# Longer rows and fewer transfers under way in a scan with a mixture of adapters

## The chip, the core and the metric

The kernel runs on one core of a Trainium2 chip. Its engines are TensorE (PE, matmuls, and PEld, the loads of their stationary operand), VectorE (DVE), ScalarE (ACT), GpSimd (POOL) and SyncE (SP), which here only issues transfers. Sixteen DMA engines move data between the chip's main memory (HBM) and the on-chip memory SBUF; matmuls write to PSUM, which has eight banks. The metric is the device time of one execution in microseconds.

## What is computed

Two stages over 8 sequences of 6400 positions with 128 features. The first is a linear recurrence along each sequence:

```python
for t in range(S):
    h = a[:, t] * h + b[:, t]
    out[:, t] = h
```

The second treats all 51,200 positions as rows `x` of 128 features. Each row picks two of 8 adapters by its logits, and adds their weighted outputs:

```python
logits = x @ w_gate                       # (N, 8)
topk = the two largest of each row; w = softmax over those two
delta[row] += w[row, k] * ((x[row] @ A[e]) @ B[e])     # A[e]: 128 x 16, B[e]: 16 x 128
return x + delta
```

Inputs a and b and the output are float32, 26.2 MB each. Every position of a and b is read once and every position of the output is written once.

## The kernel before

The rows are cut into 100 chunks of 512 positions (C), and each chunk into 4 blocks of 128 (J). A chunk goes through these steps; the short names are those of the operations in the order lists:

- `la`, `lb` (line 396): transfers of a and b from HBM into `a_tm` and `b_tm`. From chunk 4 on (HEAD) two chunks come in one transfer, laid out as `(p j) d -> p j d`: each of the 128 partitions gets 8 consecutive positions, a row of 4 KB. The first four chunks come singly, in rows of 2 KB. There are six buffers of two chunks for each input (NL).
- `P` (line 417): PE turns positions into columns, because the scan runs along the free dimension. In a pair, chunk h lies in partitions 64h to 64h+63, so its transposes use half of the array's rows. A `P` weaves the 8 half transposes of b of chunk c with the 8 of a of chunk c+1, which use the other half. They go into PSUM banks `pB` and `pA`, two of each.
- `ae` (line 435): ACT copies a from `pA` into one of three tiles `a_st` of one chunk.
- `sc` (line 482): DVE scans the chunk, from `a_st` and `pB`, into `xT` (float16, features in partitions, positions in columns; NX chunks of room).
- `Z`, `ze` (lines 500, 506): for a unit of 4 or 6 blocks, PE multiplies x by the 8 adapters' A and by the gate in one matmul of 136 columns; ACT copies the result to `zl` (room for NZ blocks).
- `g1` to `g8`, `gx`, `w1` (lines 534 to 554): DVE, POOL and ACT find the two largest logits and the weights, for a group of up to 4 units.
- `mu` (line 569): POOL, sometimes DVE, multiplies z by the weights.
- `T`, `te` (lines 578, 300): PE transposes the weighted z, and ACT or DVE copies it to `zwT`.
- `D`, `oe` (lines 588, 589, 300): PE adds x, transposed back, and the adapters' outputs in a bank of `pO`; ACT, sometimes DVE, copies it to `outt` (room for NO blocks).
- `st` (line 631): a transfer of two chunks (the last four singly) from `outt` to HBM. Which blocks an output row takes follows from the layout of the store: `xT` is read in steps so that block b holds every eighth position of a pair.

The order of the work on each engine is written out by hand-given lists, `ORDER`, one for each engine (SyncE's list holds nearly all transfers). `Program.waits` derives from them and from each operation's dependencies which semaphores it waits for. An engine does its list in order: a transfer that waits on SyncE holds up all behind it. A load waits until the transposes of the former content of its buffer are done, a store until its `oe` copies are done, and an `oe` until the former store of its place has landed. `fi` are filler transposes that only keep PE at work between chunks 7 and 14.

`SPLIT` cuts the store of chunks 68 and 69 into two transfers of 124 and 4 partitions.

Of the kernel before, what the change touches and what calls it, by code (L numbers as in the profile page):

```python
# [7 lines left out]
F32 = mybir.dt.float32  # L8
# [18 lines left out]
TAIL_CHUNKS = 12  # L27
ORDER = {
# [16 lines left out]
    ),  # L45
    "act": (
# [16 lines left out]
    ),  # L63
    "dve": (
# [14 lines left out]
    ),  # L79
    "pool": (  # L80
# [100 lines left out]
def bass_associative_scan_2x2__then__mixture_of_adapters_kernel(  # L181
# [56 lines left out]
    with ExitStack() as stack:  # L238
# [140 lines left out]
        def woven(c):  # L379
            return c >= HEAD  # L380

        def load(c, n):
            p, h = c // HC, c % HC
            sl = p % NL
            for o_l, o_t, key, tile, src in ((o_la, o_A, "la", a_tm, af), (o_lb, o_B, "lb", b_tm, bf)):
# [13 lines left out]
                for k in range(n):  # L399
                    o_l[c + k] = op  # L400
# [330 lines left out]
```

## Time and profile before

| what | value |
|---|---|
| median of 3 runs | 201.11 us (200.93 to 202.12) |
| the profiled execution | 201.01 us |
| its span, first to last instruction | 199.2 us |
| granted TensorE clock, mean | 0.994 |
| bytes read from HBM, written to it | 52.56 MB, 26.21 MB |
| mean rate of the transfers over the span | 398 GB/s |

The page of the profile gives each engine's busy time with its share of the span and its number of instructions, the span in slices, the DMA queues (packets, MB, and the time of their packets as a share of 16 engines' span), the groups of instructions by source line, and the transfers by their tiles with the median time from issue to landing. The view of stages gives the same busy times, the DMA share and the rate for any stretch of the span. The view of waits says who waited for whom, and for SyncE (SPq) what its queue waited for. "issue" is time in which an engine waited for nothing that the profile shows. A busy PE is not a PE at its peak, since matmuls overlap.

### The profile page before, as it was taken

To read this page: it belongs to the slowest core of one execution; us is meant where nothing else is said; L and a number is where in the kernel's file an instruction comes from. 1 tells how busy PE (TensorE), PEld (TensorE's weight loads), DVE (VectorE), ACT (ScalarE), POOL (GpSimd) and SP (SyncE) were. 2 spreads that over 40 slices of the span, in tenths; PEclk is the share of its full clock that TensorE was granted. 3 is DMA by queue.
4 is the path that set the end of the run, shared out by engine and by line. 5 is a ranking of instruction groups with operands and counts; after the bars stand their busy time and mean duration, and the time that the engine had idled before them with its cause. 6 is when DMAs were issued, how large, how long until landed. Compare 5 with 4: busy or idle time off the path is not lost.

```text
span 199.2 us, 7709 instructions
## 1 busy us (share of the span) xinstructions
PE 185.2 (93%) x3224; PEld 165.5 (83%) x3224; DVE 175.0 (88%) x291; ACT 176.9 (89%) x327; POOL 136.0 (68%) x168
## 2 busy tenths in 40 slices
PE   6899999999998979999999999999999999999990
PEld 6778888889987968899989989889988978878970
DVE  1599999989999879799999999999999899899980
ACT  2378699999988979899999999999999989999981
POOL 3210186878786657969989998796598978676520
PEclk9999999999999999999999999999999999999997
DMA  5999999999999999999999999999999999999796
GB/s 214 385 414 406 410 407 407 409 406 410 411 410 413 414 411 412 415 414 408 414 415 406 411 410 416 411 411 415 414 412 414 417 410 412 406 393 392 298 405 254
DMA packets 22921, 79.26 MB, mean 398 GB/s; under 512 B 2664, under 2 KB 2920, under 8 KB 22888
## 3 DMA queue, kind: packets, MB, share of 16 engines
q1 hardware_dynamic: 22312, 78.39, 98.1%
q8 instruction: 25, 0.41, 0.8%
q10 hardware_dynamic: 576, 0.40, 0.6%
q14 instruction: 8, 0.07, 0.1%
HBM read 52.56 MB, written 26.21 MB: 395 GB/s over the span
## 4 chain that ended last, share of the span: by engine, by line
PE 80%; ACT 5%; DMA 4%; issue 3%; SPq 2%; POOL 2%; DVE 1%; DVEq 0%
PE pB L417 23%; PE pO L588 13%; PE pZ L500 13%; PE pO L578 12%; PE pO L589 10%; PE pA L417 5%; DMA a_tm<-in_a_dram 4%; ACT outt L300 3%; PE pA L446 2%; SPq L396 2%; POOL zw L569 2%; ACT zwT L300 1%; ACT a_st L435 1%; ACT zl L506 1%; DVE xT L482 1%
## 5 line engine op out<-in xcount | busy, mean ns | idle before, releaser
L482 DVE TENSOR_TENSOR_SCAN xT<-a_st,xT,pB 128x512 f16<-128x512 f32 x96 | 120.4, 1254 | 6.6 <-PE pA L417 3.1
L569 POOL TENSOR_TENSOR zw<-zl,g 128x512 f16<-128x512 f32 x90 | 94.5, 1065 | 29.2 <-DVE g L554 23.2
L417 PE MATMUL pB<-ident_f,b_tm 64*128 64x64 f32 (+1 forms) x784 | 67.5, 229 | 1.2 <-issue 0.5
L417 PE MATMUL pA<-ident_f,a_tm 64*128 64x64 f32 (+1 forms) x784 | 67.8, 229 | 0.6 <-issue 0.4
L435 ACT COPY a_st<-pA 128x512 f32<-128x512 f32 x100 | 59.0, 613 | 7.9 <-PE pA L417 7.2
L417 PEld LDWEIGHTS pB<-ident_f,b_tm 64*128 64x128 f32 (+1 forms) x784 | 55.8, 139 | 10.9 <-issue 3.4
L506 ACT COPY zl<-pZ 128x816 f32<-128x816 f32 (+1 forms) x69 | 58.1, 842 | 1.7 <-PE pZ L500 1.6
L588 PE MATMUL pO<-ident_h,xT 128*128 128x128 f16 x368 | 55.2, 233 | 2.0 <-issue 1.8
L417 PEld LDWEIGHTS pA<-ident_f,a_tm 64*128 64x128 f32 (+1 forms) x784 | 56.0, 139 | 1.2 <-DMA a_tm<-in_a_dram 0.7
L300 ACT COPY outt<-pO 128x512 f32<-128x512 f32 x87 | 52.2, 609 | 4.6 <-PE pO L589 4.1
L589 PE MATMUL pO<-cst_h,zwT 128*128 128x128 f16 x368 | 53.0, 219 | 1.7 <-issue 1.7
L588 PEld LDWEIGHTS pO<-ident_h,xT 128*128 128x128 f16 x368 | 46.3, 144 | 4.9 <-issue 2.1
L589 PEld LDWEIGHTS pO<-cst_h,zwT 128*128 128x128 f16 x368 | 39.6, 108 | 1.8 <-issue 1.8
L500 PE MATMUL pZ<-cst_h,xT 128*128 128x136 f16 x400 | 37.8, 229 | 0.5 <-issue 0.4
L578 PE MATMUL pO<-ident_h,zw 128*128 128x128 f16 x368 | 35.5, 220 | 1.1 <-POOL zw L569 0.4
L500 PEld LDWEIGHTS pZ<-cst_h,xT 128*128 128x128 f16 x400 | 30.6, 145 | 1.5 <-DVE cst_h L324 0.2
L578 PEld LDWEIGHTS pO<-ident_h,zw 128*128 128x128 f16 x368 | 22.3, 97 | 5.5 <-POOL zw L569 1.3
L300 DVE COPY zwT<-pO 128x512 f16<-128x512 f16 x56 | 23.0, 414 | 3.5 <-PE pO L578 3.1
L300 ACT COPY zwT<-pO 128x512 f16<-128x512 f16 x36 | 21.4, 600 | 0.9 <-PE pO L578 0.8
L545 POOL TENSOR_TENSOR L<-L,k 128x192 f32<-128x192 f32 x14 | 8.8, 631 | 4.6 <-DVE L L543 4.0
L482 DVE TENSOR_TENSOR_SCAN xT<-a_st,pB 128x512 f16<-128x512 f32 (+1 forms) x8 | 7.5, 938 | 4.5 <-PE pB L417 4.4
L548 POOL TENSOR_TENSOR k<-k,L 128x192 f32<-128x192 f32 (+1 forms) x17 | 9.1, 535 | 2.5 <-DVE L L539 1.8
(56 smaller groups left out, 120.0 us busy)
## 6 DMA issues: line engine op xcount, KB each, us to landing
a_tm<-in_a_dram SPq DMA_DIRECT2D x48, 512.0 KB, 13.3
b_tm<-in_b_dram SPq DMA_DIRECT2D x48, 512.0 KB, 13.4
out_dram<-outt SPq DMA_DIRECT2D x47, 512.0 KB, 11.9
a_tm<-in_a_dram SPq DMA_DIRECT2D x4, 256.0 KB, 4.9
out_dram<-outt SPq DMA_DIRECT2D x4, 256.0 KB, 4.0
b_tm<-in_b_dram SPq DMA_DIRECT2D x3, 256.0 KB, 5.6
out_dram<-outt SPq DMA_DIRECT2D x1, 496.0 KB
b_tm<-in_b_dram ACTq DMA_DIRECT2D x1, 256.0 KB, 4.0
```

The lines of the kernel that those rows point to most:

```text
L300: return e.copy(dst, src) if e is eng["act"] else e.tensor_copy(dst, src)
L417: last = e.transpose(*args)
L435: lambda e: e.copy(a_st[c % NA][:, :], pA[:, c % 2, :]))
L482: last = e.tensor_tensor_scan(out=x[:, s0:s1], data0=a_st[c % NA][:, s0:s1], data1=pB[:, c % 2, s0:s1], initial=init, op0=ALU.mult, op1=AL ...
L500: last = e.matmul(pZ[:, k // (n // 2), o : o + W], xblock(b0 + k), Awg_h)
L506: lambda e: e.copy(zl[:, zb : zb + n, :].rearrange("p (h k) w -> p h (k w)", h=2), pZ[:, :, 0 : n // 2 * W]))
L545: d3 = wide(5, [d3], lambda e: e.tensor_tensor(out=ll, in0=ll, in1=kk, op=ALU.add))
L548: d6 = wide(7, [d2, d5], lambda e: e.tensor_tensor(out=kk, in0=kk, in1=ll, op=ALU.add))
L569: lambda e: e.tensor_tensor(out=wv, in0=zv, in1=gv, op=ALU.mult))
L578: last = e.transpose(ptile[:, k * 128 : k * 128 + 128], zz[:, k, :], ident_h[:, :])
L588: e.matmul(dst, xblock(b0 + k), ident_h[:, :], start=True, stop=False)
L589: last = e.matmul(dst, zt[:, k * 128 : k * 128 + 128], B_h, start=False, stop=True)
```

## The change

- **a** is loaded four chunks at a time (1 MB, rows of 8 KB: each partition holds 16 consecutive positions) into three buffers; **b** stays in pairs, in five buffers. The last four chunks (LAST) come singly, like the first four.
- In a quad, chunks k and k+1 lie in partitions 0 to 63 and chunks k+2 and k+3 in 64 to 127, and their positions alternate in runs of 8. So a half transposition (`pieces_a`, half s of a pair) holds 8-position runs of both chunks of a pair. ACT's copy `ae` writes these runs to their places in a tile `a_st` of two chunks: 64 runs of 8 elements, every other run. A scan now waits for both halves of its pair.
- A `P` weaves b of chunk c with the half of a that `partner(c)` names, up to six chunks ahead. `Y` and `X` are halves of a, and chunks of b, without a partner.
- Stores take four chunks (rows of 8 KB), but for the first four and the last four chunks. `xT` is then read in steps of 16 positions.
- `AHEAD`: each transfer on SyncE also depends on the one four places before it, so that at most four are under way.
- `xT` has room for 32 chunks (24 before), `outt` for 96 blocks (72), `zl` for 80 blocks (120). The fillers and the split store are gone. At the end the free banks of `pA` and `pB` are taken in a ring worked out from their last use.
- All five order lists are new.

```diff
-STORES = [2] * 48 + [1] * 4
-SPLIT = {68: [124, 4]}
+STORES = [2, 2] + [4] * 23 + [1] * 4
+SPLIT = {}
...
-FILL = {k: 4 for k in range(7, 15)}
+FILL = {}
 HEAD = 4
-NL = 6
 NA = 3
-NX = 24
-NZ = 120
-NO = 72
+NX = 32
+NZ = 80
+NO = 96
...
+AHEAD = 4
+LAST = 4
+NPA = 2
+NPB = 2
+NLA = 3
+NLB = 5
+NL = 6
...
     "pe": (
...
+        "wu0 wu1 wu2 wu3 wu4 wu5 wu6 wu7 wu8 wu9 wu10 wu11 A0 wu12 wu13 wu14 wu15 B0 A1 B1 A2 A3 cm B2 Z0 Y5 Y4 B3 P4 "
...
     "sp": (
...
+        "la1 lb1 la0 lb3 lb2 la2 la3 la4 lb4 la8 lb6 lb8 la12 lb10 lb12 la16 lb14 lb16 la20 lb18 lb20 la24 st0 lb24 "
+        "lb22 lb26 la28 st2 lb28 la32 lb30 st4 lb32 la36 lb34 lb38 lb36 la40 lb40 la44 lb42 st8 lb44 lb46 la48 lb48 "
...
+        "st48 la96 lb94 st52 la97 lb96 st56 lb97 st60 lb98 la98 st68 la99 lb99 st76 st64 st72 st80 st84 st88 st96 "
+        "st92 st97 st98 st99 "
...
+        for before, op in zip(self.order["sp"], self.order["sp"][AHEAD:]):
+            op.deps = op.deps + [before]
...
-    HC = 2
+    HC = 4
+    HT = HC * J
+    HP = 2 * J
...
-        a_tm = sbuf("a_tm", [128, HC * J, D], F32, NL)
-        b_tm = sbuf("b_tm", [128, HC * J, D], F32, NL)
-        a_st = sbuf("a_st", [128, C], F32, NA)
+        a_tm = sbuf("a_tm", [128, HT, D], F32, NLA)
+        b_tm = sbuf("b_tm", [128, HP, D], F32, NLB)
+        a_st = sbuf("a_st", [128, 2 * C], F32, NA)
...
+        def load(c, key):
+            o_l, o_t, tile, src, h, nl = (o_la, o_A, a_tm, af, HC, NLA) if key == "la" else (o_lb, o_B, b_tm, bf, 2, NLB)
+            n = h if woven(c) else 1
+            p, k = c // h, c % h
+            assert not (woven(c) and k)
+            view = src[c * C : (c + n) * C, :].rearrange("(p j) d -> p j d", p=128)
+            dst = tile[p % nl][:, k * J : (k + n) * J, :]
...
+        def pieces_a(c, s, dst):
+            t = a_tm[c // HC % NLA]
             if not woven(c):
                 dv = dst.rearrange("d (p j) -> d j p", j=J)
...
+            dv = dst.rearrange("d (p j) -> d j p", j=HP)
+            lo = 64 * (c // 2 % 2)
+            hi = lo + 64
+            return [(dv[:, j, :], t[lo:hi, HP * s + j, :], ident_f[lo:hi, lo:hi]) for j in range(HP)]
...
+        def tile_a(c):
+            h = c - c % 2 if woven(c) else c
+            if h not in st_of:
+                st_of[h] = turn_s[0] % NA
+                turn_s[0] += 1
+                o_ae[h] = []
+            return h, st_of[h]
...
+        def add_ae(c, s, k, o):
+            h, q = tile_a(c)
+            t = a_st[q]
+            dst, src = t[:, 0:C], pA[:, k, :]
+            if woven(c):
+                dst = t[:, :].rearrange("d (p s j) -> d s p j", s=2, j=HP)[:, s]
+                src = src.rearrange("d (p j) -> d p j", j=HP)
+            op = P.add("act", f"ae{c + s}", J, [o] + some(free_s[q]), lambda e: e.copy(dst, src))
+            free_a[k] = op
+            o_ae[h].append(op)
+
+        def half_a(c, s):
+            need(c, "la")
+            tile_a(c)
+            k, free = bank_a(c + s)
+            o = P.add("pe", f"Y{c + s}" if woven(c) else f"A{c}", HP if woven(c) else J, [o_la[c], o_id] + free,
+                      trans(pieces_a(c, s, pA[:, k, :])))
...
+        def partner(c):
+            k = c // HC * HC
+            n, s = ((k + 2, 1), (k + HC, 0), (k + HC + 2, 0), (k + HC, 1))[c % HC]
+            return (n, s) if n < NCH and woven(n) else None
...
             o_sc[c] = P.add("dve", f"sc{c}", len(segs),
-                            [o_ae[c], o_B[c]] + get(o_sc, c - 1) + xlast.get(c % NX, (0, []))[1], scan)
+                            o_ae[h] + [o] + get(o_sc, c - 1) + xlast.get(c % NX, (0, []))[1], scan)
+            free_b[k] = o_sc[c]
+            free_s[q] = o_sc[c]
```

More of the change, by code (lines that the diff above doesn't have):

```diff
@@ L379, in woven @@
         def woven(c):
[L380 to L385, printed above, removed]
-                rows = src[c * C : (c + n) * C, :]
-                if woven(c):
-                    view = rows.rearrange("(p j) d -> p j d", p=128)
-                    dst = tile[sl][:, :, :]
-                else:
-                    view = rows.rearrange("(h p j) d -> p h j d", p=128, j=J)
-                    dst = tile[sl][:, h * J : (h + n) * J, :].rearrange("p (h j) d -> p h j d", j=J)
-                op = P.add(
-                    "act" if c == 0 and key == "lb" else "sp", f"{key}{c}", n,
-                    get(o_t, HC * (p - NL)) + get(o_t, HC * (p - NL) + HC - 1),
-                    lambda e, dst=dst, view=view: e.dma_start(dst, view),
-                    sem=dma_sem(f"{key}{sl}" if n == HC else f"{key}x{c}"),
-                )
-                for k in range(n):
-                    o_l[c + k] = op
@@ L405, in pieces, with need @@
+        def need(c, key):
+            if c not in (o_la if key == "la" else o_lb):
+                load(c - c % (HC if key == "la" else 2) if woven(c) else c, key)
+        def pieces_a(c, s, dst):
+            t = a_tm[c // HC % NLA]
             if not woven(c):
                 dv = dst.rearrange("d (p j) -> d j p", j=J)
-                return [(dv[:, j, :], t[:, h * J + j, :], ident_f[:, :]) for j in range(J)]
-            dv = dst.rearrange("d (p j) -> d j p", j=HC * J)
-            lo, hi = 64 * h, 64 * h + 64
@@ L410, in pieces, with pieces_b @@
-            return [(dv[:, j, :], t[lo:hi, j, :], ident_f[lo:hi, lo:hi]) for j in range(HC * J)]
-        def trans(*which):
+                return [(dv[:, j, :], t[:, c % HC * J + j, :], ident_f[:, :]) for j in range(J)]
+            dv = dst.rearrange("d (p j) -> d j p", j=HP)
+            lo = 64 * (c // 2 % 2)
+            hi = lo + 64
+            return [(dv[:, j, :], t[lo:hi, HP * s + j, :], ident_f[lo:hi, lo:hi]) for j in range(HP)]
+        def pieces_b(c, dst):
+            t = b_tm[c // 2 % NLB]
+            if not woven(c):
+                dv = dst.rearrange("d (p j) -> d j p", j=J)
+                return [(dv[:, j, :], t[:, c % 2 * J + j, :], ident_f[:, :]) for j in range(J)]
+            dv = dst.rearrange("d (p j) -> d j p", j=HP)
+            lo = 64 * (c % 2)
+            hi = lo + 64
+            return [(dv[:, j, :], t[lo:hi, j, :], ident_f[lo:hi, lo:hi]) for j in range(HP)]
@@ L413, in f, with trans @@
+        def trans(*lists):
             def f(e):
-                lists = [pieces(*w) for w in which]
                 for group in zip(*lists):
@@ L437, in load_next @@
-        def load_next(c):
-            if c < NCH and c not in o_la:
-                load(c, 1 if c < HEAD else HC)
-        o_fi = {}
-        def filler(c):
-            def f(e):
-                for _ in range(FILL[c]):
-                    last = e.transpose(pA[:, c % 2, 0:128], ident_f[:, :], ident_f[:, :])
-                return last
-            if c in FILL:
-                o_fi[c] = P.add("pe", f"fi{c}", FILL[c], get(o_ae, c - 2) + [o_id], f)
-        def front(c):
-            load_next(c)
+        turn_a, free_a = [0], [None] * NPA
@@ new lines, in bass_associative_scan_2x2__then__mixture_of_adapters_kernel, with some, bank_a, f @@
+        turn_b, free_b = [0], [None] * NPB
+        turn_s, free_s = [0], [None] * NA
+        o_fi, st_of = {}, {}
+        def some(o):
+            return [o] if o is not None else []
+        def tile_a(c):
[5 more added lines that the diff above has]
+            return h, st_of[h]
+        def bank_a(name):
+            k = turn_a[0] % NPA
+            turn_a[0] += 1
+            free = some(free_a[k])
+            if name in FILL:
+                def f(e):
+                    for _ in range(FILL[name]):
+                        last = e.transpose(pA[:, k, 0:128], ident_f[:, :], ident_f[:, :])
+                    return last
+                free = [P.add("pe", f"fi{name}", FILL[name], free + [o_id], f)] + free
+            return k, free
@@ L456, in front @@
[L456 to L469 removed]
+                half_a(c, 0)
@@ new lines, in front @@
+                o = P.add("pe", f"B{c}", J, deps, trans(part))
+            else:
+                if c == HEAD:
+                    for n, s in ((c, 0), (c, 1), (c + 2, 0)):
+                        half_a(n, s)
+                to = partner(c)
+                if to is None:
+                    o = P.add("pe", f"X{c}", HP, deps, trans(part))
+                else:
+                    n, s = to
+                    need(n, "la")
+                    tile_a(n)
+                    ka, free = bank_a(n + s)
+                    o = P.add("pe", f"P{c}", HP, deps + [o_la[n]] + free, trans(part, pieces_a(n, s, pA[:, ka, :])))
+                    o_A.setdefault(n, []).append(o)
+                    add_ae(n, s, ka, o)
@@ L471, in front @@
+            o_B[c] = [o]
+            h, q = tile_a(c)
             x = xcols(c)
+            at = a_st[q][:, (c - h) * C : (c - h + 1) * C]
             r0 = c * C
```

68 lines of the change are left out of this document (27 added, 41 removed), and 114 rows, old and new, of the table ORDER.

## The prediction

> **What bounds the kernel now.** I read the page first, then the DMA rows, and only then the engines' waits.
>
> ```profile
> span 199.2 us, 7709 instructions
> PE 185.2 (93%) x3224; PEld 165.5 (83%) x3224; DVE 175.0 (88%) x291; ACT 176.9 (89%) x327; POOL 136.0 (68%) x168
> ...
> DMA packets 22921, 79.26 MB, mean 398 GB/s; under 512 B 2664, under 2 KB 2920, under 8 KB 22888
> ...
> q1 hardware_dynamic: 22312, 78.39, 98.1%
> ```
>
> No compute engine is full over the span, though four of them come near it. The main DMA queue (q1) is full: its packets took 98.1% of the time of 16 engines. The stages of the span show when:
>
> ```profile
> core 0: us, PE busy (x) PEld busy (x) DVE busy (x) ACT busy (x) POOL busy (x), PEclk, DMA share, GB/s
> 1.00:2.00 1.00, 0.33 (x2) 0.34 (x3) 0.35 (x2) 0.00 (x0) 0.37 (x2) 1.00 0.00 0
> 2.00:3.00 1.00, 1.00 (x6) 1.00 (x5) 0.21 (x2) 0.87 (x1) 0.00 (x0) 1.00 0.76 280
> ...
> 40.00:160.00 120.00, 115.51 (x2170) 104.89 (x2167) 111.88 (x159) 114.77 (x210) 97.88 (x117) 1.00 1.03 412
> ...
> 184.00:188.00 4.00, 3.93 (x67) 3.76 (x65) 4.00 (x18) 4.00 (x10) 1.78 (x4) 1.00 0.70 274
> ```
>
> The last two columns are the DMA share and the rate. For 120 us the queue stands at a share of 1.03 and 412 GB/s (a share over 1 means that packets overlap a little). At that rate the 79.26 MB alone need 192.4 of the 199.2 us. What is left is the start (no byte before 2 us), a dip to 274 GB/s between 184 and 188 us, and the drain. So the transfers bound the kernel. ACT (114.77 of 120, 96%) and DVE (93%) follow so closely that they are the next bound, and in the dip both are at 4.00 of 4: there the DMA waits for them.
>
> All times below are for the profiled execution (span 199.2, whole time 201.01 us, so 1.8 us lie around the span); the median of the runs, 201.11, is the same within 0.1%.
>
> **The longer rows.** Their price must come from rows of two lengths. First the main queue between 100 and 116 us, where only 4 KB rows move; then between 195.6 and 197.4 us, where only single-chunk stores in 2 KB rows move:
>
> ```profile
> q1 hardware_dynamic: 1792, 6.52, 101.4%
> ```
>
> ```profile
> q1 hardware_dynamic: 375, 0.68, 99.0%
> ```
>
> The columns are packets, MB and share of 16 engines. In the first, 1.014 x 16 x 16 us = 259.6 us of engine time moved 6.52 MB. One engine's sixteenth of a 512 KB transfer (32,768 bytes) so takes 1.305 us, its completion included. In the second, 0.99 x 16 x 1.8 = 28.5 us moved 0.68 MB: a sixteenth of 256 KB takes 0.687 us. Half the bytes cost more than half the time: 2 x 0.687 - 1.305 = 0.069 us do not depend on the length. A 1 MB transfer in 8 KB rows would by the same line take 1.305 + 2 x (1.305 - 0.687) = 2.541 us, where two 512 KB transfers take 2.610.
>
> The change makes 23 such loads of a (chunks 4 to 95, 46 pair loads before) and 23 such stores: 46 x 0.069 = **-3.2 us**. The 0.68 is rounded to 0.005, which moves the 0.069 by 0.010, so -2.7 to -3.6 on that line. No row shows 8 KB packets on this queue; if time goes by bytes alone above 4 KB, the saving is nothing. I take the line's value, since two lengths lie on it.
>
> The Trainium skill, in *DMA: Bandwidth & Descriptors*, section "Why small descriptors are slow", puts the fixed part at about 3 cycles of 32 bytes per packet, 131 cycles instead of 128 for 4 KB. By that, 8 KB rows would save about 1.1% and not the 2.6% that the rows above give; the trace, with 0.069 us a pair, speaks for the larger.
>
> **The last four chunks one by one.** Loads of a and b for chunks 96 to 99 come as 8 transfers of 256 KB instead of 4 of 512 KB: 8 x 0.687 - 4 x 1.305 = **+0.3 us**. The store that went as 124 and 4 rows is now part of a whole one; its bytes are the same. How these rows were spread is not shown: between -1.3 and +1.3 us (one pair's 1.305 on an engine), taken as 0.
>
> **Four under way: the head.** Each SyncE transfer now waits until the one four places earlier has landed. Here are the issues of before at the start, and the page's rows of time to landing:
>
> ```profile
> 0.74 0.38 SPq L396 DMA_DIRECT2D a_tm<-in_a_dram  x1
> 1.17 0.42 SPq L396 DMA_DIRECT2D b_tm<-in_b_dram  x1
> 1.64 0.90 SPq L396 DMA_DIRECT2D a_tm<-in_a_dram  x2
> ...
> a_tm<-in_a_dram SPq DMA_DIRECT2D x48, 512.0 KB, 13.3
> ...
> a_tm<-in_a_dram SPq DMA_DIRECT2D x4, 256.0 KB, 4.9
> ```
>
> From an issue at 0.74 to the first bytes after 2.0 us lie about 1.4 us. In the head all transfers are 256 KB, so four hold 1.05 MB, 2.5 us at 412 GB/s. When one lands, 1.9 us of work are left, and SyncE needs to wake, issue (0.4) and reach the first bytes (1.4): nearly all the cover is used for the eight head transfers. No row shows this limit; it costs between nothing and 8 x 0.4 = 3.2 us, if the issue is never hidden. I take **+0.8**, a quarter, because the ACT queue's own load and constants run beside it. In the new order a0 stands third on SyncE and b0 fourth on ACT, and PE's B3 stands behind the first quad, la4, of 1 MB. So the first scans start up to 1 us later; this lies on DVE, below.
>
> **Four under way: the rest.** Before, 13.3 us to landing at 412 GB/s are 5.5 MB, some ten transfers under way. Now a, b, b and a store are 3.1 MB or 7.6 us. When the oldest lands, 2.1 to 2.6 MB (5.1 to 6.4 us) are left, well over 1.8 us for the next issue and first bytes. In steady flow: nothing. What it loses is the cover for a SyncE that stands still behind a store:
>
> ```profile
> 67.19 0.91 SPq L396 DMA_DIRECT2D a_tm<-in_a_dram  x2
> 76.62 0.34 SPq L631 DMA_DIRECT2D out_dram<-outt  x1
> ...
> 46.37 0.82 SPq L631 DMA_DIRECT2D out_dram<-outt  x2
> ...
> SPq L631 <- ACT outt L300: 23.3, 13, 5.0
> ...
> SPq L631 <- ACT sd L549: 12.9, 4, 8.8
> ```
>
> Before, SyncE issues nothing from 68.1 to 76.6 us, and the queue carries it. The new order's first whole store, st4, stands after la32 and lb30. It needs chunk 7's output, as the pair stores at 46.37 did. Issued ahead of it are 36 chunks of a, 32 of b and 4 of the output, 72 x 0.262 = 18.9 MB: at 412 GB/s they last until 2.3 + 45.8 + 0.8 = 48.9 us. The cover at 46.4 is 2.5 us, against 1.8 needed. For this and its like I take **+0.3**; bounds are nothing and the second rival.
>
> **The engines.** Would they follow a queue that ends earlier? From the orders: ACT loses 7 of its copies to zwT (38 to 31) and gains 2 of outt (95 to 97); DVE takes the 7 and gives up 2 of outt. 32 filler transposes are gone.
>
> ```profile
> L300 ACT COPY zwT<-pO 128x512 f16<-128x512 f16 x36 | 21.4, 600 | 0.9 <-PE pO L578 0.8
> L300 ACT COPY outt<-pO 128x512 f32<-128x512 f32 x87 | 52.2, 609 | 4.6 <-PE pO L589 4.1
> L300 DVE COPY zwT<-pO 128x512 f16<-128x512 f16 x56 | 23.0, 414 | 3.5 <-PE pO L578 3.1
> L300 DVE COPY outt<-pO 128x512 f32<-128x512 f32 x5 | 3.4, 674 | 0.5 <-PE pO L589 0.5
> L435 ACT COPY a_st<-pA 128x512 f32<-128x512 f32 x100 | 59.0, 613 | 7.9 <-PE pA L417 7.2
> L506 ACT COPY zl<-pZ 128x816 f32<-128x816 f32 x62 | 53.7, 867 | 1.1 <-PE pZ L500 1.0
> L588 PEld LDWEIGHTS pO<-ident_h,xT 128*128 128x128 f16 x368 | 46.3, 144 | 4.9 <-issue 2.1 <-DVE zwT L300 0.6 <-ACT zwT L300 0.4
> L588 PEld LDWEIGHTS pA<-ident_h,xT 128*128 128x128 f16 x16 | 1.9, 129 | 0.3 <-ACT zwT L300 0.3
> L446 PE MATMUL pA<-ident_f 128*128 128x128 f32 x32 | 5.0, 279 | 0.0
> ```
>
> ACT: -7 x 0.600 + 2 x 0.609 = -3.0 us, to 173.9. DVE: +7 x 0.414 - 2 x 0.674 = +1.5, to 176.5. PE loses 5.0 us of filler, which lay in early idle time: nothing gained. ACT, the fullest from 40 to 160 us, so drops by as much as the queue is to gain. DVE would stand at about (111.88 + 0.9) of 118.5, 95%, and its late start comes out of its idle time. On the path: 0, as long as the orders keep DVE fed; the third case says what if not.
>
> ACT now writes a in 64 runs of 8 elements. A copy over two runs costs (867 - 613) / (816 - 512) = 0.84 ns an element, so one break costs nothing visible. I take 613 again; the nearest row in which steps do cost is PE's load of xT (144 ns, against 129 where the step is half). If each of 92 copies grew by that share (12%), ACT would gain 6.8 us and be full. The same xT load now steps twice as far: from nothing to 15 ns more on each of 736 (11 us on PEld, which is 83% busy and overlaps PE). I take 0.
>
> **The tail.** Between 184 and 188 us the dip costs 4 x (412 - 274) / 412 = 1.3 us. In the new order st76, st64 and st72 (3.1 MB, 7.6 us) stand behind the last load, two of them long ready, and the last b is a single chunk that reaches its scan without a pair partner. I take half, **-0.7** (0 to -1.3).
>
> Sum: -3.2 + 0.3 + 0.8 + 0.3 - 0.7 = -2.5 us, so 201.0 - 2.5 = **198.5 us**.
>
> **Rivals.** *The rows are worth less, or are cut.* If 8 KB rows go out as 4 KB packets, or time goes by bytes, -3.2 becomes 0: 201.7. If the length-free part is mostly the completion of a transfer and not its packets, the saving lies between, and so does the time. By the page cited above it would be 1.1% of 2.610, 0.03 us for each of 46, -1.4 in all, and the time 200.3. For it: no row shows 8 KB on this queue. Against it: two lengths and one line.
>
> *SyncE stands behind stores that are not ready* (the slower side). The place is the 23 stores of four chunks: each waits for four outputs, and no load behind it can pass. With a full window of 7.6 us less the 1.8 of restarting, a standstill longer than 5.8 us idles the queue by what is over. The 8.5 us of before would cost 2.7 us each; when the window is half drained (3.8 us), 6.5. Before had four waits of the ACT sd kind and 13 of the outt kind, longest 8.8 and 5.0. Three such at a full window cost 8.1, which makes 206.6; one half-drained one alone makes 205.0. It decides above 2.5 us in sum, one standstill of 8.3 us. For it: before stood still this long. Against it: the order was made anew, with fewer issues.
>
> *DVE becomes the bound.* Its scans start 1 us later with 1.5 us more to do; if its idle time stays as it is, the whole end moves by that and nothing of the queue's gain is seen: 201.0 + 2.5 = 203.5; half of it taken up, 202.3.
>
> **How the numbers follow.** Forecast 0.50 (own range 196.7 to 199.5); rows worth less 0.12; DVE 0.15; standstill 0.23. About 1% (2 us) is what a measurement of this kernel can tell from no change. The forecast lies for nine tenths below 199.0: faster 0.47. Its rest and most of the first and third cases are within 1%: 0.28; slower is the standstill and the worst of DVE: 0.25. The range takes the forecast, both middle cases and the mild end of the standstill: 196.5 to 203.8.
>
> **What would show it.** In the new profile q1 should have about 16,300 packets and near 419 GB/s from 40 to 160 us (3.1 MB took an engine 6 x 1.305 = 7.83 us and should take 2 x 2.541 + 2 x 1.305 = 7.69: 412 x 7.83 / 7.69). A rate of 412 there means that rows save nothing. Slices well under 400 in the middle mean standstills, and the rows of SyncE's waits name the store. If the queue is short of work with SyncE waiting for PE's transposes, an engine is the bound. A dip at the end as before makes the -0.7 wrong; a first scan later than 7.6 us makes the head dearer than taken.

## The result: 3% slower, and where the time went

The changed kernel takes 208.16 us (median of 4 runs, 206.47 to 211.24), the kernel before 201.02 us beside it. The ratio is 1.0305, with a 95% interval of 1.0211 to 1.0399. Medians, here and below, are over all runs of a kernel, and ratios with their intervals leave out executions in the chip's slower state (here the one of 211.24 us), so it is the ratios that are compared: 1.0305 is 6.1 us, where the medians differ by 7.1. The time is above the forecast range, on the side of the rivals.

The profiled execution of the changed kernel took 209.54 us. These lines of its page answer to those shown of before: the rate in 40 slices, the packets, the queue, the chain that ended last by engine, and three rows of the transfers (count, size, median us to landing).

```profile
span 207.5 us, 7580 instructions
...
GB/s 185 323 426 409 414 399 392 276 381 402 370 411 369 360 418 394 415 343 302 406 430 408 399 414 408 419 420 383 416 402 339 414 355 390 403 383 428 414 409 254
DMA packets 16881, 79.26 MB, mean 382 GB/s; under 512 B 2000, under 2 KB 2256, under 8 KB 10960
...
q1 hardware_dynamic: 16272, 78.39, 96.4%
...
DMA 64%; PE 22%; ACT 6%; DVE 4%; issue 1%; ACTq 1%; SPq 0%
...
a_tm<-in_a_dram SPq DMA_DIRECT2D x23, 1024.0 KB, 7.9
b_tm<-in_b_dram SPq DMA_DIRECT2D x46, 512.0 KB, 7.4
out_dram<-outt SPq DMA_DIRECT2D x23, 1024.0 KB, 7.4
```

The long rows are there: 16,272 packets, as forecast. The time to landing is what four transfers should take (7.6 us forecast). But the rate has holes in the middle of the span (276, 343, 302, 339, 355), which before had not, and the chain that ended last now runs for 64% of the span through transfers. The stage that held 412 GB/s before shows it in one row:

```profile
core 0: us, PE busy (x) PEld busy (x) DVE busy (x) ACT busy (x) POOL busy (x), PEclk, DMA share, GB/s
40.00:160.00 120.00, 113.71 (x2150) 103.47 (x2149) 111.31 (x160) 112.33 (x207) 97.05 (x118) 1.00 1.00 391
```

391 GB/s, where 419 was forecast if rows save and 412 if they save nothing. Who kept the queue short says the view of waits for SyncE (who waited for whom, us in total, times, longest):

```profile
SPq L399 <- DMA a_tm<-in_a_dram: 41.9, 22, 3.5
SPq L399 <- DMA b_tm<-in_b_dram: 32.6, 37, 2.2
SPq L717 <- DMA out_dram<-outt: 16.6, 9, 2.2
SPq L399 <- DMA out_dram<-outt: 12.8, 6, 3.5
SPq L678 <- DMA a_tm<-in_a_dram: 10.6, 7, 3.2
SPq L717 <- ACT outt L307: 10.0, 3, 5.9
```

The first five rows (115 us) are transfers waiting for the landing of earlier ones, that is, the limit of four. Stores that wait for ACT's outputs, the rival's cause, come only after them.

### The profile page after: what moved, and what is told of

It reads as the page before. It is cut to its first block, busy times and chain, and to the rows that moved or that the text cites. A ratio compares the mean times of both kernels' runs of the same rounds, so it can differ in the third digit from the quotient of the medians.

```text
span 207.5 us, 7580 instructions
## 1 busy us (share of the span) xinstructions
PE 187.1 (90%) x3160; PEld 168.0 (81%) x3160; DVE 176.9 (85%) x294; ACT 175.9 (85%) x323; POOL 135.8 (65%) x170
## 3 DMA queue, kind: packets, MB, share of 16 engines
q1 hardware_dynamic: 16272, 78.39, 96.4%
## 4 chain that ended last, share of the span: by engine, by line
DMA 64%; PE 22%; ACT 6%; DVE 4%; issue 1%; ACTq 1%; SPq 0%
DMA b_tm<-in_b_dram 32%; DMA a_tm<-in_a_dram 25%; PE pB L433 8%; DMA out_dram<-outt 7%; PE pZ L549 3%; PE pA L433 3%; PE pO L627 3%; PE pO L637 2%; ACT outt L307 2%; PE pO L638 2%; ACT zl L555 1%; ACT a_st L473 1%; DVE zw L618 1%; DVE zwT L307 1%; ACTq L323 1%
## 5 line engine op out<-in xcount | busy, mean ns | idle before, releaser
L529 DVE TENSOR_TENSOR_SCAN xT<-a_st,xT,pB 128x512 f16<-128x512 f32 x96 | 120.4, 1254 | 10.7 <-PE pA L433 6.0
L433 PE MATMUL pB<-ident_f,b_tm 64*128 64x64 f32 (+1 forms) x768 | 68.8, 235 | 8.8 <-DMA b_tm<-in_b_dram 3.7
L433 PE MATMUL pA<-ident_f,a_tm 64*128 64x64 f32 (+1 forms) x768 | 69.7, 236 | 1.4 <-DMA a_tm<-in_a_dram 1.3
L473 ACT COPY a_st<-pA 128x512 f32<-128x512 f32 x100 | 60.3, 619 | 12.4 <-PE pA L433 12.0
L307 ACT COPY outt<-pO 128x512 f32<-128x512 f32 x91 | 54.6, 609 | 7.6 <-PE pO L638 6.9
L433 PEld LDWEIGHTS pA<-ident_f,a_tm 64*128 64x128 f32 (+1 forms) x768 | 57.8, 144 | 2.0 <-DMA a_tm<-in_a_dram 1.9
L307 DVE COPY zwT<-pO 128x512 f16<-128x512 f16 x64 | 26.1, 409 | 3.3 <-PE pO L627 3.1
L307 ACT COPY zwT<-pO 128x512 f16<-128x512 f16 x28 | 17.0, 607 | 0.9 <-PE pO L627 0.6
L597 POOL TENSOR_TENSOR k<-k,L 128x192 f32<-128x192 f32 (+2 forms) x16 | 9.0, 560 | 8.8 <-DVE L L588 8.4
L591 POOL TENSOR_TENSOR k<-zl,m 128x192 f32<-128x192 f32 (+1 forms) x14 | 7.0, 502 | 8.8 <-DVE m L590 8.8
L594 POOL TENSOR_TENSOR L<-L,k 128x192 f32<-128x192 f32 (+2 forms) x15 | 8.9, 595 | 5.7 <-DVE L L592 5.0
```

Source lines behind the costliest of these rows:

```text
L307: return e.copy(dst, src) if e is eng["act"] else e.tensor_copy(dst, src)
L433: last = e.transpose(*args)
L473: op = P.add("act", f"ae{c + s}", J, [o] + some(free_s[q]), lambda e: e.copy(dst, src))
L529: last = e.tensor_tensor_scan(out=x[:, s0:s1], data0=at[:, s0:s1], data1=pB[:, k, s0:s1], initial=init, op0=ALU.mult, op1=ALU.add,)
L594: d3 = wide(5, [d3], lambda e: e.tensor_tensor(out=ll, in0=ll, in1=kk, op=ALU.add))
L597: d6 = wide(7, [d2, d5], lambda e: e.tensor_tensor(out=kk, in0=kk, in1=ll, op=ALU.add))
```

## Experiments

Theory at the start: the limit of four starves the queue. Rivals: the later first scans (new order at the head); the missing fillers; quads that come late; engines that set the end. All runs, with medians in us and ratios to the kernel before:

| run | what it is | median | ratio (95%) |
|---|---|---|---|
| changed | | 208.16 | 1.0305 (1.0211 to 1.0399) |
| e1_no_limit | changed, no limit | 203.95 | 1.0109 (1.0075 to 1.0143) |
| e4_eight | changed, limit of eight | 204.09 | 1.012 (1.007 to 1.0171) |
| e2_before_four | before, limit of four | 230.49 | 1.1376 (1.1292 to 1.1461) |
| e14_before_eight | before, limit of eight | 202.10 | 1.0045 (1.0024 to 1.0066) |
| e3_head_order | changed, first scan early | 208.99 | 1.0359 (1.0313 to 1.0406) |
| e5_head_free | e1, head of before | 203.03 | 1.0069 (1.0041 to 1.0098) |
| e8_fill_only | changed, fillers | 208.71 | 1.032 (1.0244 to 1.0396) |
| e6_head_fill | e5, fillers | 205.33 | 1.0204 (1.0158 to 1.025) |
| e7_last_loads | e6, last loads earlier | 206.30 | 1.0157 (1.009 to 1.0224) |
| e9_quad_loads | before's orders, quads of a | 355.05 | 1.7638 (1.7527 to 1.775) |
| e10_quad_stores | before's orders, quad stores | 240.30 | 1.1959 (1.1869 to 1.205) |
| e11_quads_old_orders | before's orders, both | 393.92 | 1.9375 (1.9206 to 1.9543) |
| e12_stores_later | e5, first stores later | 203.93 | 1.009 (1.0049 to 1.0132) |
| e13_more_b | e12's idea, seven b buffers | 202.24 | 1.0033 (1.0001 to 1.0064) |
| e15_eight_singly | e13, eight chunks singly | 205.44 | 1.0121 (1.0091 to 1.0151) |
| e16_sigmoid_early | e13, sigmoid and scans early | 202.62 | 1.0051 (1.0014 to 1.0088) |
| e17_sigmoid_singly | e15, the same | 204.99 | 1.016 (1.0108 to 1.0212) |
| e18_after_sigmoid_early | changed, the same | 209.77 | 1.0321 (1.0265 to 1.0377) |

### The limit

The limit is one constant; in the kernel before, the same two lines were added.

```diff
-AHEAD = 4
+AHEAD = 200        # e1; 8 in e4
```

```diff
+AHEAD = 4          # e2, in the kernel before; 8 in e14
...
+        for before, op in zip(self.order["sp"], self.order["sp"][AHEAD:]):
+            op.deps = op.deps + [before]
```

> The changed kernel with the limit of four transfers lifted (AHEAD = 200), all else the same. Theory L (the limit costs the time: landings in the head and the cover behind stores): the rate from 40 to 160 us goes from 391 to 412 or more, 419 if 8 KB rows save what two lengths of rows gave, the fourth scan starts 2 us earlier, and the time falls from about 208 to 200-202. Theory O (the new orders, stores of four chunks and the missing fillers cost it): the time stays at 205 or more.

> The kernel before with one thing of the change: each SyncE transfer also waits for the one four places earlier. Transfers there are half as large, so four hold 2.1 MB or less (5.1 us) instead of 13.3 us. Theory L: 206 to 212 us, with slices well under 400 GB/s. Theory O: within 2 us of 201.

> The changed kernel with eight transfers under way instead of four (AHEAD = 8). Theory L: near the run without a limit, within 1 us. If a deep queue costs something of its own (loads landing late behind stores), this is faster than both four and no limit. Theory O: no change from 208.

> The kernel before with each SyncE transfer waiting for the one eight places earlier: 4.2 MB under way at most, where four were 2.1 MB (230.5 us), the changed kernel's four some 3.1 MB (its limit cost 4 us) and its eight about 6 MB (nothing). If what counts is the bytes that wait behind the slowest of the 16 engines, it costs between: 1 to 4 us, 202 to 205. If it is the number of transfers, eight cost nothing: 201 to 201.5.

Without the limit the changed kernel needs 203.95 us, with eight 204.09: the limit of four costs about 4 of the 6 us (by the ratios, 1.0305 to 1.0109), and eight are as good as none. In the kernel before, four cost 28 us (230.49 against 202.10 beside it) and eight 0.8 (202.10 against 201.30). One row of e2, columns as above (the middle of the span, engines, clock, share and rate):

```profile
40.00:160.00 120.00, 106.81 (x1949) 96.66 (x1949) 102.07 (x145) 104.68 (x188) 87.48 (x106) 0.97 0.99 363
```

What the limit does to the queue is not mostly idle time. These are its rows from 40 to 160 us (packets, MB, share of 16 engines), before, e2, e1 and the changed kernel:

```profile
q1 hardware_dynamic: 13493, 49.14, 101.5%
```

```profile
q1 hardware_dynamic: 11890, 43.30, 98.0%
```

```profile
q1 hardware_dynamic: 9373, 49.06, 100.5%
```

```profile
q1 hardware_dynamic: 8916, 46.60, 99.4%
```

From before to e2 the bytes fall by 12%, the share of the engines only by 3%: a MB takes 43.5 us of engine time instead of 39.7. From e1 to the changed kernel the bytes fall by 5%, the share by 1%, and a MB takes 41.0 us instead of 39.3. Most packets are as short as before (the median of a 4 KB packet is 159 ns before and in e2), but a few are much longer: over 280 ns took 367 of 10,569 in e2, and 40 of 11,995 before. Whether an engine works or waits within such a packet, the records do not tell.

The price falls with the bytes that may be under way. By transfer sizes: before with four 2.1 MB (28 us), changed with four 3.1 MB (4 us), before with eight 4.2 MB (0.8 us), changed with eight about 6 MB (nothing). The number of transfers alone does not order these (four cost 28 and 4). That bytes are the measure is a reading of four points in two kernels, which also differ in their orders and rows.

The runs also show what the rows are worth. The main queue between 100 and 150 us, first before, then e1, where it is full:

```profile
q1 hardware_dynamic: 5628, 20.49, 101.6%
```

```profile
q1 hardware_dynamic: 3816, 20.64, 100.6%
```

Sixteen engines for 50 us at 1.016 moved 20.49 MB, 39.7 us of engine time for a MB; with the long rows 39.0, which is 1.7% less. The forecast had 7.83 to 7.69, 1.8%. For all 78.4 MB, shared by 16 engines, that is the 3 us of the forecast.

### The head, the fillers, the last loads

Of the order lists, the diffs here show only the entries around a change.

```diff
# e3, in the changed kernel: SyncE, then ACT, then DVE
-la1 lb1 la0 lb3
+la0 lb1 la1 lb3
-cb cw ca lb0
+ca lb0 cb cw
-ch ih own pk sc0 sc1
+own ih pk sc0 ch sc1
# e5, in e1: the first entries of before on SyncE, ACT, DVE and PE
+la0 lb1 la1 la3 lb2 la2 lb3
# ... (the lists of ACT, DVE and PE likewise)
# e6, in e5, and e8, in the changed kernel: 32 filler transposes between Z1 and P12
+FILL = {k: 4 for k in range(8, 16)}
# e7, in e6
-la98 st68 la99 lb99 st76
+la98 la99 lb99 st68 st76
```

> The changed kernel with four under way, but the first transfers placed as before: a0 first on SyncE, b0 second on ACT ahead of two of the constants, and VectorE's conversion of the gate's constants behind the first scan. The first scan starts at 9.3 us in the changed kernel and at 6.6 in the kernel before. If the place of b0 sets the head: first scan at 7 to 7.5, fifth 2 us earlier, time 2 us lower (206). Theory L: the first scan comes earlier but the fifth by under 1 us, since the first load of four chunks still waits its turn; time 207 to 208.

> No limit, and the head of the kernel before: a0 first, b0 second on ACT, PE's B3 and A3 ahead of the first halves of the quad, the constants' conversion behind the second scan. Without a limit alone the sixth scan (sc5) starts at 17.4 us against 14.8 in the kernel before, and the time was 1.1% above it. If the head is what is left: sc5 at 14.5 to 15.5, the dip of the rate between 30 and 45 us (328 GB/s) shallower, time 200 to 202. If the new orders and the stores of four chunks are: sc5 earlier, but the time stays at 203 to 204.

> The run before plus four filler transposes ahead of each P from 5 to 12. In the changed kernel the granted clock fell to 0.5 in one slice after 20 us, and in the run without a limit too. If the missing fillers cost time by the clock: no slice below 0.9 and 0.5 to 1.5 us less than without them. If not: within 0.3 us, the fillers lying in idle time as the prediction has it.

> The run before plus the last two loads (a99, b99) issued ahead of the store st68 instead of behind it. Without a limit b99 landed at 180.2 us and its scan started at 184.2. If the last loads hold the end: 1 to 2 us less. If the engines hold it (ACT and DVE full to the end): within 0.5 us.

> The changed kernel as it is, four under way, with the same fillers and nothing else. If the clock's drop costs: 1 to 2 us below 208, no slice at 0.5. Theory L: the time is set by transfers, and stays at 207 to 209 though the clock holds.

The first scan starts at 6.60 us before, 9.30 in the changed kernel, 6.94 in e3 and 6.26 in e5. In e3 nothing of it reaches the end; its scan of chunk 5 (sc5) starts at 21.8 us, later than in the changed kernel (19.4). Without the limit the earlier head is worth about 0.9 us (203.95 to 203.03), but the intervals of the two ratios overlap. Fillers give nothing with the limit (e8) and cost 2 us without it (e6). They were to hold the granted clock, which in the changed kernel is 0.50 from 20 to 25 us, and do not do so reliably: one slice of the pages stands at 0.5 in e6, at 0.6 in e8. In the execution of e7 that was traced no slice is below 0.9, and it took 203.77 us, so a held clock alone does not bring the time back. The last load of a landing 3 us earlier (e7, 177.2 against 180.5) gives nothing that can be told from e6. So the 2 us that e5 still loses are somewhere else.

### The orders of before with longer rows

Here the quads were to be tried one by one with the order lists of before, changed only where an operation would otherwise wait for one behind it.

```diff
# e9, e11: a in quads, b in five pairs, no limit, lists of before (not shown)
# e9
-STORES = [2, 2] + [4] * 23 + [1] * 4
+STORES = [2] * 48 + [1] * 4
# e10, in the kernel before
-STORES = [2] * 48 + [1] * 4
+STORES = [2, 2] + [4] * 23 + [1] * 4
```

> The orders, pair stores and rooms of the kernel before; only a comes in quads (three buffers, b in five pairs), without the limit of four. What is open is the 2 to 3 us by which the changed kernel without its limit (203.95) and with the head of before (203.03) stays above before (201.0). If quads of a make the early chunks late, this run keeps that cost: sc5 at about 17 us and 202.5 to 203.5 us. If quad stores or the new orders are the cause, it is at or under before: 199.5 to 201 us (23 loads save some 0.7 to 1.6 us), with sc5 under 16 us.

> The kernel before with its pair loads and orders, but stores of four chunks. A store of four chunks reads xT in steps of 16, so the first block of a quad can be worked on only after the scan of its fourth chunk; two such places of PE's list had to move. If that is the cause, outputs come later, SyncE stands behind them, and the time is 202.5 to 204 us. If quad loads or the new orders are, it is 199.5 to 201 us.

> Both: a in quads and stores of four chunks, no limit, all orders those of the kernel before as far as the longer dependencies let them stand. If the new orders are the cause, 198.5 to 200.5 us (both row savings, 1.3 to 3.2 us). If one of the quads is, what that one's run shows, 202.5 to 204 us; if each brings a part, the two differences to before add up here.

None of the theories had this: 355, 240 and 394 us. The view of waits of e9 shows where it stands:

```profile
SPq L397 <- PE pA L431: 176.4, 30, 13.9
...
PE pB L431 <- ACT a_st L471: 97.2, 66, 2.3
PEld pB L431 <- issue: 90.0, 59, 2.4
```

Halves of a are now taken up to six chunks ahead, and three buffers of a come free only when a whole quad is used. In lists timed for pairs, SyncE waits for PE, PE for ACT's copy of a and ACT for work that stands behind those. In e10, which keeps a in pairs, the longest wait of PE is another one, 32.3 us for VectorE's scans ahead of `Z` (21 times). The granted clock is lower too, 0.77 in e9 against 0.99 before, with PE busy for 232.8 us instead of 185.2. These runs say that quads need orders of their own; they do not say what the quads cost, and leave the question of the 2 us open.

### The dry stretch at 30 to 45 us

The stage from 30 to 45 us (last column: GB/s), before, e5 and then e13:

```profile
30.00:45.00 15.00, 14.07 (x269) 12.51 (x268) 13.78 (x18) 14.76 (x27) 11.76 (x14) 1.00 1.03 408
```

```profile
30.00:45.00 15.00, 14.30 (x266) 12.55 (x264) 14.23 (x18) 14.67 (x28) 10.56 (x14) 1.00 0.97 351
```

```profile
30.00:45.00 15.00, 14.34 (x262) 12.59 (x263) 14.23 (x18) 14.67 (x27) 10.31 (x13) 1.00 1.02 411
```

e5 moves 351 GB/s there, before 408. The timeline of SyncE in e5 (start, us, what):

```profile
27.86 0.33 SPq L399 DMA_DIRECT2D a_tm<-in_a_dram  x1
34.18 0.35 SPq L678 DMA_DIRECT2D out_dram<-outt  x1
34.57 2.58 SPq L399 DMA_DIRECT2D b_tm<-in_b_dram  x3
37.19 0.43 SPq L399 DMA_DIRECT2D a_tm<-in_a_dram  x1
40.95 0.34 SPq L678 DMA_DIRECT2D out_dram<-outt  x1
```

From 28.2 to 34.2 us it stands behind the first store, and loads whose buffers are free stand behind it.

```diff
# e12, in e5, on SyncE
-la24 st0 lb24 lb22 lb26 la28 st2 lb28 la32 lb30 st4 lb32 la36
+lb22 la24 lb24 la28 st0 lb26 lb28 la32 lb30 st2 lb32 la36 lb34 st4
# e13, in e5: two more buffers, and more loads of b ahead of st0 and st2
-NX = 32
+NX = 28
-NLB = 5
+NLB = 7
-lb16 la20 lb18 lb20 la24 st0 lb24 lb22 lb26 la28 st2 lb28 la32 lb30 st4 lb32 la36 lb34 lb38 lb36 la40 lb40
+lb16 lb18 la20 lb20 lb22 lb24 la24 lb26 la28 lb28 lb30 st0 la32 lb32 lb34 st2 la36 lb36 lb38 la40 st4 lb40
```

> The changed kernel with the head of before and no limit (203.03 us), and in SyncE's list st0, st2 and st4 put behind the loads whose buffers come free while SyncE stands at them (22 to 34 us: lb22, lb24, la28; 37 to 41: lb28, la32, lb30; 43 to 49: lb32, la36, lb34). If the loss left over is that dry stretch of 30 to 45 us (351 GB/s, against 408 before: 0.86 MB or 2.1 us), it fills to over 390 GB/s and the time falls by 1 to 2 us to 201 to 202. If late work on the engines sets the end whatever the transfers do, the stretch fills and the time stays within 0.7 of 203.

> The same with seven buffers of b pairs instead of five (room of xT 28 chunks instead of 32), and two more loads of b ahead of st0 and st2. If the stretch is dry because the loads may not lead far enough, it fills wholly (405 GB/s and more) and the time goes to 200 to 201.5 us, under the run with the order alone by 0.5 or more. If not, equal to that run.

The order alone brings the stretch to 400 GB/s and no time. With two more buffers of b it is full (e13, 411) and the median falls to 202.24, 0.3% above before (0.0 to 0.6%). From 20 to 170 us the queue of e13 is then as full as before, in longer rows; its last load of b lands at 177.0 us, before at 178.2. Yet the end comes no earlier.

### Why the full queue ends no earlier

The execution of e13 that was traced took 201.09 us, 1.15 under its median and as long as that of before (201.01). So its trace can show where the gain of the longer rows goes, but not the 0.3%.

VectorE by stages, before and then e13 (busy us with instructions, clock, DMA share, GB/s):

```profile
core 0: us, DVE busy (x), PEclk, DMA share, GB/s
7.00:20.00 13.00, 11.73 (x21) 1.00 1.03 411
45.00:160.00 115.00, 107.64 (x153) 1.00 1.03 412
160.00:190.00 30.00, 28.11 (x74) 1.00 0.96 385
```

```profile
7.00:20.00 13.00, 8.58 (x17) 0.92 1.02 415
45.00:160.00 115.00, 110.08 (x160) 1.00 1.02 414
160.00:190.00 30.00, 28.94 (x81) 1.00 0.94 382
```

VectorE of e13 does 3.2 us less from 7 to 20 us and works that off until 190 us, at 96% in both later stages where before had 94%. Its scans have caught up long before: that of chunk 50 starts at 88.0 us, before at 91.1. Two causes of the late start were tried: quads that land late (e15), and an entry of the lists that the forecast had passed over: the change moved `sg`, a sigmoid on ScalarE that only brings its table, from the start to behind `ae32`, and put `g8_0` ahead of `sc5`. The timelines of ScalarE and VectorE in the changed kernel:

```profile
17.12 0.59 ACT L473 COPY a_st<-pA 128x512 f32<-128x512 f32 x1 [1.14 <-PE pA L433]
17.72 1.28 ACT L598 ACT_TABLE_LOAD   x1
19.02 0.23 ACT L598 ACTIVATE sd<-k 128x32 f32<-128x32 f32 x1
```

```profile
19.28 0.19 DVE L603 SCALAR_TENSOR_TENSOR g<-L,sd 128x32 f32<-128x32 f32 x1 [0.60 <-ACT sd L598]
19.39 1.27 DVE L529 TENSOR_TENSOR_SCAN xT<-a_st,xT,pB 128x512 f16<-128x512 f32 x1
```

The scan of chunk 5 (19.39) stands behind the weights, these behind the first sigmoid, and that behind a table load of 1.28 us. The Trainium skill, *ScalarE: Activation LUTs*, section "What ACT_TABLE_LOAD costs", gives 1283 ns for the load, which agrees, and about 1380 ns of draining beside it, which this trace does not show: the copy ahead ends at 17.71 and the sigmoid starts at 19.02.

```diff
# e15, in e13 (lists of PE, ACT and SyncE follow)
-HEAD = 4
+HEAD = 8
# e16 in e13, e17 in e15, e18 in the changed kernel
-ae32 sg oe10
+ae32 oe10
+lb0 cb sg cw        # e18: lb0 sg
-sc4 g8_0 sc5 g1_1 sc6 g4_1 sc7 g8_1 sc8 sc9
+sc4 sc5 g8_0 g1_1 sc6 sc7 g4_1 sc8 g8_1 sc9
```

> The run with seven b buffers (202.24 us), and the first eight chunks loaded singly instead of four: quads and pairs begin with chunk 8. In that run the queue was full again to 170 us, and yet the end came no earlier than before; VectorE worked 8.6 of the 13 us from 7 to 20 us (before 11.7), made 2.4 up to 160 us and was full to the end. If the quads' late first chunks (sc5 at 16.6 us, before 14.8) cost the end because VectorE never makes them up, sc5 comes to 15 to 15.5, VectorE works 10.5 or more of the 13 us, and the time falls 1 to 2 us, to 200.2 to 201.2, at or under before. If VectorE's or the end's own order is what holds (the last scans to the last output take 12.7 us, before 11.2), the start is better and the time stays within 0.5 of 202.2.

> The run with seven b buffers (202.24 us), with two places of the orders as in the kernel before: sg, a sigmoid on ScalarE that brings its table, back at the start (the change had put it behind ae32, so a second table load of 1.28 us stands ahead of the first w1), and the scans sc5 and sc7 ahead of g8_0 and g4_1 on VectorE instead of behind them. If that is what makes the early chunks late, sc5 comes from 16.6 to 15.2 us, sc10 from 25.7 to under 24, and the end by 1 to 2 us: 200.2 to 201.3. If the loads of a quad are what they wait for, nothing: 201.8 to 202.7.

> The same two places undone in the run with eight chunks loaded singly (205.44 us). If the sigmoid and the gating ahead of the scans hold the early chunks, sc5 is at 14.9 and the time 1 to 2 us under 205.4, still above the run with quads, since that run's own loss, a transfer queue that stands still at 170 to 175 us, stays. If loads and order each held them in turn, more than 2 us are gained here and under 0.5 in the run with quads.

> The changed kernel (208.16 us, four under way) with those two places alone undone. If they cost the end, 206 to 207.2 us; if the limit of four hides them, since there the early loads come later anyway, 207.6 to 208.7.

Both theories of the early chunks fell. e15 brought the loads earlier (b of chunk 6 lands at 13.6 us instead of 16.2), and sc5 stayed at 16.7, behind that sigmoid; the time rose by 3 us in the medians, 1.8 by the ratios, and its queue stood at 250 GB/s from 170 to 180 us. e16 had VectorE at 10.7 of the 13 us, sc5 at 16.0 instead of 16.6, sc8 at 20.3 instead of 22.0, and ended no earlier (202.62 against 202.24); e17 and e18 do not differ from e15 and the changed kernel by more than the intervals. A VectorE that starts earlier is stopped again later: by the scan of chunk 15 (33.0 us in e16, 33.1 in e13) the lead is gone.

What stays is the end. These are VectorE's scan of chunk 95 and ACT's last copy to `outt` in e13:

```profile
167.30 1.28 DVE L529 TENSOR_TENSOR_SCAN xT<-a_st,xT,pB 128x512 f16<-128x512 f32 x1
```

```profile
194.53 0.58 ACT L307 COPY outt<-pB 128x512 f32<-128x512 f32 x1 [1.32 <-PE pB L638]
```

From the one to the other are 27.2 us. In eleven runs with the new end, with and without the limit, with other heads, buffers and last loads, this time is 27.20 to 27.25 us (e1, e3 to e7, e12, e13, e15 to e17); in others with four under way it is longer, 27.4 in e8 and 27.7 in the changed kernel. Before it was 24.6 (169.70 to 194.26), in e14 25.1. From the scan of chunk 99, the last, it is 12.6 to 12.7 us in all fourteen runs with the new end and 11.2 before and in e14, and at that scan 86 copies to `outt` are done both in e13 and before. It does not follow the transfers: e7 has the last loads earlier, and 27.22. The stage itself, before and then e13 (all engines: PE, PEld, DVE, ACT, POOL):

```profile
169.70:194.30 24.60, 23.61 (x363) 20.57 (x360) 22.51 (x72) 23.36 (x49) 13.96 (x15) 1.00 0.95 378
```

```profile
167.30:194.50 27.20, 25.76 (x362) 22.93 (x359) 25.77 (x76) 24.31 (x49) 15.89 (x18) 1.00 0.91 370
```

VectorE has 3.3 us more to do there and is 95% busy, PE is too. The chain that ended last, followed back through these stages (share of the stage by engine and line), before and then e13:

```profile
by line: PE pO L578 17.0%; ACT outt L300 14.2%; PE pO L588 13.6%; PE pO L589 9.5%; PE pB L417 9.0%; PE pZ L500 6.8%; PE pA L588 3.8%; PE pB L588 3.5%; issue 3.3%; DVE outt L300 2.9%; PE pB L578 2.8%; PE pB L589 2.8%; PE pA L589 2.7%; ACT zl
```

```profile
by line: PE pO L637 14.3%; DVE zw L618 9.8%; ACT outt L307 9.6%; PE pO L627 9.4%; PE pO L638 9.0%; DVE zwT L307 6.5%; PE pZ L549 6.2%; DVE g L603 4.7%; DVE xT L529 4.4%; issue 3.5%; PE pA L433 3.3%; PE pB L433 3.3%; ACT zl L555 2.8%; DVE v
```

Both lines end there in the view. In the rows named, the chain passes through VectorE for 3% of the stretch before and for 25% in e13. By the lists VectorE still has 16 copies to `zwT` after that scan where it had 13, 9 products `mu` instead of 8 and 2 copies to `outt` instead of 1; with the rows of before (0.414, 0.684 and 0.674 us) that is 2.6 us. The new order lets the scans run further ahead of the outputs (at the scan of chunk 50, 28 copies to `outt` are done in e13 and 32 before; at that of chunk 95, 75 and 76), and what they leave comes near and after the last loads. So e13's scan of chunk 95 is 2.4 us earlier than before, its last output 0.3 us later. The end's order was not undone by itself: that this order, and not another part of the change, sets the 27.2 us, is read from the traces and not from an experiment.

## Why the prediction was wrong

- **"In steady flow: nothing"** is the step that failed. That the limit costs, and how much, is shown: 4 us by e1 and e4, where the term was +0.3 with the standstills. The sum was near in its sizes (7.6 us under way, 7.4 to 7.9 measured to landing; 5.1 to 6.4 us left when the oldest lands, 3.7 to 7.8 measured, median 6.1). What failed is the step from them to "nothing": that a queue with more left than a restart takes runs at its full rate. It does not: a MB took 4% more engine time than without the limit (41.0 against 39.3 us). Why is open. One candidate is that the sum took the 16 engines as one, and the next transfer starts only when the last engine has landed its part. The completion marks of one transfer (first to last engine, transfers from 40 to 160 us) lie a median of 3.7 us apart before, 2.3 in the changed kernel and 2.0 in e2, and at most 4.2 in the changed kernel, which could leave the fastest engine less than the 1.8 us of a restart. But the marks show that as rare: after the landing that lets the next transfer go, the first engine ends the youngest of the four 3.3 us later in the median, and less than 1.8 us later for 3 of 61 transfers (in e2 2.3 us, and 9 of 82). The Trainium skill, *DMA: Bandwidth & Descriptors*, section "Why a DMA increments its semaphore by 16 and not by 1", says that a transfer's engines finish independently and only the full count means landed; the marks agree.
- **Four under way, the head (+0.8).** The first scan was 2.7 us later, not up to 1, and sc5 4.6 us. Of this at most about 0.9 us reached the end, and only without the limit (e3, e5).
- **The longer rows (-3.2)** held, packets and price (1.7% of the queue's time, 1.8% forecast). The rival that they are worth less fell. They moved the queue's end forward and not the kernel's.
- **The engines (0).** The terms held one by one: the strided copy of a took 619 ns (613 taken), DVE has 176.9 us (176.5 forecast), fillers gave nothing. ACT has 175.9 instead of 173.9, 1.3 of it the second table load, which was passed over. Wrong was the place of DVE's added work: the forecast spread it over a span with idle time, and it stands in the last 27 us.
- **The tail (-0.7)** has the wrong sign: +2.6 us from the scan of chunk 95 to the last output. The changed kernel has 401 GB/s from 184 to 188 us, but ends 8 us later; in e13, with the queue full until 170 us, the dip is back (323 and 349 GB/s in its slices from 184 to 194 us) though the last loads are in. That it is a sign of the engines' end and not a cost of its own is argued from this.
- **The rivals.** The slower one gave 206.6 by the wrong cause: in the changed kernel SyncE waited 6.3 and 10.0 us for ACT's outputs, and over 110 for the limit. Its mechanism does exist without the limit: the standstill of 28 to 34 us. "DVE becomes the bound" comes nearest to what is left once the limit is gone and the stretch full; that it had 202.3 to 203.5 and e13 has 202.2 is partly luck, since it moved the whole end by the late first scans, and those were made up by chunk 50.

Together, by the ratios: of the 6.1 us above before, 3.9 are the limit, 0.8 the head, 0.7 the dry stretch, and 0.7 (0.0 to 1.3) stay, beside the 3 us of the rows that the end takes back. Only the limit's part is clear of the intervals. No version beat the kernel before.

## What to carry over

Bytes under way over the rate, less the time of a restart, is not enough to size a limit on transfers: by that sum 3 MB cost nothing here. Measured, 2 MB cost 28 us, 3 MB 4 and 4 MB still 0.8. A saving on a full queue is only worth what the engines behind it can end earlier, so look at the last stretch, from the last loads to the last output, and count which work a new order leaves for it. And read every entry of a new order list, also those that compute nothing for the result, such as one that only brings a table.

## What was unexpected of the hardware

- The 16 engines' parts of one transfer landed up to 5.7 us apart (before, 40 to 160 us; median 3.7), and a limit of transfers holds them closer (2.0 in e2) at the price of the rate (363 against 412 GB/s). Most of that price stands in the records as packets that take longer (43.5 us of engine time a MB against 39.7), and not as engines without a packet.
- A copy of 512 elements in 64 runs of 8 costs ScalarE 619 ns against 613 in one run, and the load of x in steps of 16 instead of 8 positions the same 144 ns.
